# Extra score tiles through a cubic on GpSimd and VectorE, taken across segment borders, in a two-layer attention and MLP kernel

## The chip, the cores and the metric

The kernel runs on one core of a Trainium2 chip. The core's engines work at once, each through its own queue in order: TensorE (PE) for matrix products, ScalarE (ACT) for table functions, VectorE (DVE) and GpSimd (POOL) for elementwise work, SyncE (SP) for issuing DMAs. The metric is the device time of one execution in microseconds. Before the change the median of 3 runs is 1077.08 us (1075.46 to 1078.64).

## What is computed

Two layers, each an attention block and a mixer block, with residual sums around them; batch 1, sequence S = 2048, width D = 448, 16 heads of 28, inner width 1792, all in bf16.

```python
def _A_ref(x, wqkv, wo):                       # attention
    qkv = (x @ wqkv).reshape(B, S, 3, H, Dh).transpose(2, 0, 3, 1, 4)
    q, k, v = qkv[0], qkv[1], qkv[2]
    p = softmax(einsum("bhqd,bhkd->bhqk", q, k) * Dh ** -0.5)
    return einsum("bhqk,bhkd->bhqd", p, v).transpose(0, 2, 1, 3).reshape(B, S, D) @ wo

def _B_ref(x, w1, w2, w3, w4):                 # token mixer and MLP
    h = gelu(layernorm(x) @ w1)
    x1 = x + shift_four_groups(h, by=(1, -1, 2, -2)) @ w2
    return x1 + gelu(layernorm(x1) @ w3) @ w4

x = x + _A_ref(layernorm(x), A_wqkv, A_wo)
x = x + _B_ref(layernorm(x), B_w1, B_w2, B_w3, B_w4)
x = x + _A_ref(layernorm(x), A_wqkv, A_wo)     # the same weights again
x = x + _B_ref(layernorm(x), B_w1, B_w2, B_w3, B_w4)
```

Every score must go through an exponential: 2 x 16 x 2048 x 2048 of them. They are the heart of the change.

## The kernel before

**A planner writes the order.** The kernel is a set of Python generators (tasks) that yield operations with an estimated duration, and requests for resources: PSUM banks, scratch slots, events. A planner (`Sched`) simulates the five engines with these estimates, picks the next operation by start time and priority, and so fixes each engine's instruction order; waits between engines are semaphores. On the chip each engine follows its list. When PE would idle, the planner puts in filler matmuls (L1863) that keep the array busy and its clock up; `SC.idle_share(8.0)` is the share of filler in the last 8 us of the plan.

**Scores.** A segment (`segs`) is one query chunk, one group of four heads and a run of key tiles; there are 64, in the order of `ORDER`. In chunks 0 to 2 a query chunk has 512 columns and a key block (`kb`) is one key tile of 128; in chunks 3 and 4 it has 256 columns and a block holds two key tiles. Each block has four score tiles of 128x512, one a head: 2048 tiles in both layers. A segment of chunk 0 in layer 0 has 4, 4 and 8 blocks, one of chunks 1 and 2 has 16; in layer 1 chunks 0 and 1 are cut to 7, 4 and 5 blocks, chunk 2 has 16.

`t_scores` takes the tiles in order in units of alternately three and two, computes them on PE (L1292) into banks 0 to 2 or 3 to 4, and `t_exp` has ACT take the exponential of a whole unit in one instruction (L1447) into a slot of `PT`. `t_pv` multiplies with the values (`vaug`), two key blocks at a time, in order (L753), then VectorE copies the sum out (L1526, L1528) and `t_norm` divides by the row sums (L1541, L1552 and DMAs).

**Extra tiles.** A unit may carry one or two tiles more, taken from a block 5 or 6 ahead (`DLO`, `DHI`) of the same segment, if there is at least 3% filler (`FTH`), if the segment's share is not used up (`D_RATE` x 4 x blocks so far), and if a bank of b6 and b7, one of two `yd` slots and one of four `PD` slots are free at once. Such a tile goes to VectorE: `d_first` scales it out of PSUM to a fixed-point integer whose upper half is the exponent and whose lower half is the fraction (L1333), `d_chain` evaluates a cubic of the fraction in three instructions (L1354, L1356, L1358) with an fp32 buffer of `fb`, and a fourth (L1361) puts the exponent into the bits of the bf16 result in `PD`.

**Value slots.** `vaug` has 23 slots. Layer 0 uses 0 to 15; layer 1 uses 16 to 22 for key tiles 0 to 6 and 0 to 8 for the rest, so that its first keys and values can be computed while layer 0 runs. Slots 9 to 15 also hold the inner activations of two-tile MLP groups of layer 1.

**Other work on GpSimd and VectorE.** VectorE evacuates all projections from PSUM (L1102 keys, L1135 queries, L1180 values, L1813 MLP) and does normalisations; GpSimd squares keys and queries (L1088), computes row statistics (L945 to L947, L1627 to L1639, L1757, L1759), starts the gelu of the mixer (L1694, followed by L1695 to L1697 on VectorE and ACT), multiplies the attention output (L1552) and adds residuals (L1768).

The cost that the planner uses for a VectorE tile:

```python
DST = [('dve', 0.6), ('dve', 0.6), ('dve', 0.34), ('dve', 0.6)]
```

Of the kernel before, what the change touches and what calls it, by code (L numbers as in the profile page):

```python
# [511 lines left out]
DPRIO = 5  # L512
DST = [('dve', 0.6), ('dve', 0.6), ('dve', 0.34), ('dve', 0.6)]
DLO = 5
# [5 lines left out]
PE_NORM = {(0, 0): False, (0, 1): False, (0, 2): False, (0, 3): False, (0, 4): False, (1, 0): False, (1, 1): False, (1, 2): False, (1, 3): False, (1, 4): True}  # L520
# [24 lines left out]
def build_kernel(nc, A_x, A_wqkv, A_wo, B_x, B_w1, B_w2, B_w3, B_w4, out, n_layers=2):  # L545
# [20 lines left out]
    E0, E1, E2, E3 = 0.99992525, 0.69583285, 0.22606939, 0.07802301  # L566
    NPD = 4
# [56 lines left out]
    with st:  # L624
# [73 lines left out]
        RTN, TMP, T2, RIN = (sc[:, i, :] for i in range(4))  # L698
# [142 lines left out]
        def t_setup_pool():  # L841
# [13 lines left out]
            yield op("pool", 0.2, lambda e: e.memset(astat0[:, :], 0.0), writes=[("astat0",)])  # L855
            yield ("sig", ("ind",))
# [328 lines left out]
        def t_kv(L, c):  # L1185
            t0, n = KC[L][c]
            if L == 1 and c >= 2:
                yield ("wait", ("kvfree",))
            if L == 1 and c >= FASTKV:
# [136 lines left out]

        PDS = ["pd%d" % i for i in range(NPD)]
        YS = ["y0", "y1"]

        def d_first(blk, bank, ys, pd):  # L1330
            w = num1(ys)
            y = yd[:, w, :]
            yield op("dve", c_ps(512), lambda e: e.tensor_scalar(out=y, in0=ps[:, bi(bank), :], scalar1=SCALE * L2E * FS, scalar2=-126.0 * FS, op0=ALU.mult, op1=ALU.max),  # L1333
                     reads=[("ps", bi(bank))], writes=[("yd", w)], touch=[bank])
            yield ("rel", bank)
            yield ("spawn", d_chain(blk, ys, pd), DPRIO)

        at = [0, 0]

        def d_chain(blk, ys, pd):  # L1340
            si, kb, _ = blk
            w, s = num1(ys), home[blk][1]
            y = yd[:, w, :]
            lo = y.bitcast(U16).rearrange("p (n two) -> p n two", two=2)[:, :, 0]
            hi = y.bitcast(I16).rearrange("p (n two) -> p n two", two=2)[:, :, 1]
            pdt = PD[:, s, :]

            def urge():
                return 1.0 if at[0] > si or (at[0] == si and at[1] >= kb - DURG) else DPRIO

            fr = yield ("acq", FB, [("yd", w)])
            fk = ("fb", num1(fr))
            q = fb[:, num1(fr), :]
            yield op(DST[0][0], DST[0][1], lambda e: e.scalar_tensor_tensor(out=q, in0=lo, scalar=E2 / E3 * FS, in1=lo, op0=ALU.add, op1=ALU.mult),  # L1354
                     reads=[("yd", w)], writes=[fk], urge=urge)
            yield op(DST[1][0], DST[1][1], lambda e: e.scalar_tensor_tensor(out=q, in0=q, scalar=E1 / E3 * FS * FS, in1=lo, op0=ALU.add, op1=ALU.mult),  # L1356
                     reads=[("yd", w), fk], writes=[fk], urge=urge)
            yield op(DST[2][0], DST[2][1], lambda e: e.tensor_scalar(out=pdt, in0=q, scalar1=E3 / FS ** 3, scalar2=E0, op0=ALU.mult, op1=ALU.add),  # L1358
                     reads=[fk], writes=[("pd", s)], urge=urge)
            yield ("rel", fr)  # L1360
            yield op(DST[3][0], DST[3][1], lambda e: e.scalar_tensor_tensor(out=pdt.bitcast(I16), in0=hi, scalar=128.0, in1=pdt.bitcast(I16), op0=ALU.mult, op1=ALU.add),  # L1361
                     reads=[("yd", w), ("pd", s)], writes=[("pd", s)], urge=urge)
# [3 lines left out]
        def t_scores():  # L1366
# [9 lines left out]
            while pos < len(stream):  # L1376
# [23 lines left out]
                si, kb0, _ = un[-1]  # L1400
                at[0], at[1] = si, kb0
                L, ch, g = segs[si][0:3]
                nkb = len(seg_kb[si])
                rate = DRATE(L, ch, g)
                if rate and CHUNKS[L][ch][1] == 4 and SC.idle_share(8.0) >= FTH:
                    for kb in range(kb0 + DLO, min(kb0 + DHI, nkb)):
# [3 lines left out]
                        if taken.get(si, 0) >= rate * (kb + 1) * 4:  # L1410
                            continue
                        if any(("k", L, g, kc_of(L, kt)) not in SC.events for kt in seg_kb[si][kb]):
                            break
                        got = yield ("try", [MISC[0:2], YS, PDS])
# [3 lines left out]
                        home[blk] = ("pd", int(got[2][2:]))  # L1418
                        taken[si] = taken.get(si, 0) + 1
# [39 lines left out]
        def t_pv():  # L1459
            yield ("wait", ("start",))  # L1460
            yield ("acq", ["b5"])
            for si in range(len(segs)):
# [7 lines left out]
                for k0 in range(0, len(kbs), PVB):  # L1470
# [6 lines left out]
                    for kb in batch:  # L1477
                        for i, kt in enumerate(kbs[kb]):
                            vs = vslot(L, kt)
                            for j in range(4):  # L1480
                                key, s = home[(si, kb, j)]
                                buf = PD if key == "pd" else PT
# [4 lines left out]
                        for j in range(4):  # L1487
                            key, s = home[(si, kb, j)]
                            if key == "pd":
                                yield ("rel", "pd%d" % s)  # L1490
# [198 lines left out]
        def t_tanh(L, t0, grp, z, NW, hk):  # L1689
            yield ("wait", ("hz", L, t0, grp))  # L1690
            fr = yield ("acq", FB, hk)
            fk = ("fb", num1(fr))
            f = fb[0:112, num1(fr), 0:NW]
# [4 lines left out]
            yield ("rel", fr)  # L1698
            yield ("sig", ("hA", L, t0, grp))

# [71 lines left out]
        def t_mixB(L, tiles, direct, pr):  # L1772
# [20 lines left out]
            elif side:  # L1793
                yield ("wait", ("kvfree",))
# [6 lines left out]
            late = []  # L1801
            for fch in range(14):
# [5 lines left out]
                if direct or ("tail",) in SC.events:  # L1808
# [6 lines left out]
                yield ("spawn", later([ev], b, [("h2", L, tiles[0], fch)]), 1.5)  # L1815
            yield ("rel", x_)
            for fch in range(14) if not direct else ():
                yield ("wait", ("h2", L, tiles[0], fch))
# [5 lines left out]
            for i, t in enumerate(tiles):  # L1824
# [4 lines left out]
                for fch in range(14):  # L1829
                    if direct:  # L1830
                        yield ("wait", ("h2", L, tiles[0], fch))
# [69 lines left out]
        SC.spawn(t_third(), 3)  # L1901
        SC.spawn(t_final(), 9)
# [58 lines left out]
```

## Time and profile before

| | |
|---|---|
| median of 3 runs | 1077.08 us |
| the profiled execution | 1079.42 us, span 1077.7 us, mean granted clock 0.995 |
| instructions on VectorE, ACT, GpSimd | 1234, 919, 506 |
| GpSimd's two-input rows of 512 columns (mean) | L1552 1308 ns, L1694 1244 ns, L1088 1074 and 1050 ns |
| GpSimd's row statistics | 209 to 615 ns each |
| exponentials of three tiles, of two | 1548 ns x402, 1126 ns x402 (they overlap each other) |
| layer 1's first key projection, evacuated by VectorE | 272.98 to 284.03 us |
| layer 1's second one | 420.22 to 436.15 us |

In the profile's rows "busy" is the union of a group's spans and the mean is one instruction's duration. In the table of stretches each row has a stretch, its length, busy time and count of PE, PE's weight loads, DVE, ACT and POOL, the granted clock, the DMA share and GB/s. Lines are those of the kernel's file.

### The profile page before, as it was taken

The numbers are of one execution on the slowest core, as the hardware profiler recorded it, in microseconds if no ns is written. First come the engines' busy times: TensorE is split into PE (matmuls) and PEld (weight loads), VectorE is DVE, ScalarE is ACT, GpSimd is POOL, SyncE is SP. The second block draws the span as 40 slices with busy tenths as digits, with TensorE's granted clock in tenths as the row PEclk, the third lists the DMA queues.
The fourth block names the chain that finished last, engine by engine and source line by source line (L and its number), as shares of the span: only waits on it lengthen the run. The fifth ranks groups of instructions, "written<-read, shape, count | busy, mean of one in ns | idle before, by whom it ended". The sixth has DMA issues, their size and how long they took to land.

```text
span 1077.7 us, 35124 instructions
## 1 busy us (share of the span) xinstructions
PE 1006.0 (93%) x15918; PEld 420.7 (39%) x15921; DVE 637.4 (59%) x1234; ACT 1017.9 (94%) x919; POOL 312.7 (29%) x506
## 2 busy tenths in 40 slices
PE   6899999999999999899999999999999999999998
PEld 2333443443333344343433333343333433444464
DVE  8776679836568526766356643515695394554551
ACT  6898999999999999999999999999999999999951
POOL 2244125301254014452032201102743030432130
PEclk9999999999999999999999999999999999999999
DMA  4547221103111022220221132423311110220000
GB/s 114 138 111 211 78 56 33 27 12 91 32 31 32 12 70 65 49 36 23 43 77 41 43 93 84 132 69 100 79 27 22 46 36 12 53 58 16 12 11 33
DMA packets 92614, 62.26 MB, mean 58 GB/s; under 512 B 64688, under 2 KB 82368, under 8 KB 92464
## 3 DMA queue, kind: packets, MB, share of 16 engines
q1 hardware_dynamic: 89088, 51.92, 18.7%
q0 software_dynamic: 3376, 8.09, 2.7%
q8 instruction: 125, 2.05, 0.8%
q14 instruction: 25, 0.20, 0.1%
HBM read 27.12 MB, written 15.71 MB: 40 GB/s over the span
## 4 chain that ended last, share of the span: by engine, by line
ACT 73%; PE 17%; DVE 6%; DMA 2%; issue 1%; POOL 1%; SPq 0%; DVEq 0%
ACT PT L1447 66%; PE ps L762 10%; PE ps L1292 4%; ACT h2T L1822 4%; PE ps L753 3%; ACT fb L1696 1%; ACT L1822 1%; DMA rT<-ub 1%; ACT L1447 1%; DVE fb L1356 1%; DVE rT L1541 0%; DVE yd L1333 0%; DVE PD L1361 0%; DVE fb L1354 0%; DMA PT<-in_A_wqkv_dram 0%
## 5 line engine op out<-in xcount | busy, mean ns | idle before, releaser
L1447 ACT ACTIVATE PT<-ps 128x1536 bf16<-128x1536 f32 (+1 forms) x805 | 921.7, 1336 | 17.9 <-PE ps L1292 17.1
L1292 PE MATMUL ps<-qT,kT 32*128 32x512 bf16 (+1 forms) x2560 | 315.2, 340 | 33.2 <-ACT PT L1447 24.0
L753 PE MATMUL ps<-PT,vaug 128*32 128x512 bf16 (+1 forms) x2523 | 251.8, 342 | 0.0
L1292 PEld LDWEIGHTS ps<-qT,kT 32*128 32x128 bf16 x2560 | 80.7, 91 | 309.5 <-ACT PT L1447 279.9
L1863 PE MATMUL ps<-ident 128*32 128x256 bf16 x3688 | 165.3, 274 | 3.7 <-POOL ident L842 1.5
L762 PE MATMUL ps<-xT,w 128*32 128x512 bf16 (+2 forms) x1600 | 127.7, 360 | 2.6 <-DVE h2T L1813 1.6
L1863 PEld LDWEIGHTS ps<-ident 128*32 128x32 bf16 x3688 | 105.0, 96 | 31.0 <-issue 11.9
L1813 DVE CAST h2T<-ps 128x512 bf16<-128x512 f32 (+2 forms) x112 | 67.9, 606 | 81.0 <-PE ps L762 73.7
L762 PE MATMUL ps<-w,h2T 128*32 128x448 bf16 x1512 | 103.1, 360 | 10.2 <-ACT h2T L1822 9.8
L753 PEld LDWEIGHTS ps<-PT,vaug 128*32 128x32 bf16 x2523 | 74.5, 95 | 94.6 <-issue 81.5
L1552 POOL TENSOR_TENSOR otn<-ub,fb 128x512 bf16<-128x512 f32 (+1 forms) x36 | 40.3, 1119 | 175.6 <-DMA fb<-rscr 172.5
L1088 POOL TENSOR_TENSOR sq<-kT 128x512 bf16<-128x512 bf16 (+2 forms) x32 | 30.0, 939 | 121.5 <-DVE kT L1102 120.9
L1694 POOL TENSOR_TENSOR fb<-hT 112x512 f32<-112x512 bf16 (+1 forms) x36 | 37.7, 1049 | 83.3 <-DVE hT L1676 73.5
L762 PEld LDWEIGHTS ps<-xT,w 128*32 128x32 bf16 (+1 forms) x1600 | 44.2, 95 | 41.8 <-issue 19.3
L762 PEld LDWEIGHTS ps<-w,h2T 128*32 128x32 bf16 x1512 | 41.7, 97 | 45.8 <-issue 16.4
L1768 POOL TENSOR_TENSOR x_res<-x_res,x1b 128x448 f32<-128x448 f32 x32 | 40.2, 1262 | 23.9 <-DVE xn L959 23.8
L1333 DVE TENSOR_SCALAR yd<-ps 128x512 int32<-128x512 f32 x37 | 24.9, 679 | 32.9 <-PE ps L1292 32.7
L1541 DVE RECIPROCAL rT<-rT 16x128 f32<-16x128 f32 (+1 forms) x36 | 33.5, 932 | 17.1 <-DMA rT<-ub 17.1
L762 PE MATMUL ps<-kT,w 128*32 128x512 bf16 (+2 forms) x576 | 40.0, 360 | 2.5 <-DVE qT L1164 1.4
L1822 ACT ACTIVATE h2T<-h2T 128x7168 bf16<-128x7168 bf16 (+2 forms) x8 | 42.0, 5244 | 0.1
L1526 DVE COPY ub<-ps 128x512 f32<-128x512 f32 (+1 forms) x40 | 23.3, 582 | 30.7 <-PE ps L753 30.1
L762 PE MATMUL ps<-xT,wq_pad 128*32 128x512 bf16 x448 | 40.2, 396 | 0.6 <-DVE kmaxc L1113 0.3
(164 smaller groups left out, 1168.3 us busy)
## 6 DMA issues: line engine op xcount, KB each, us to landing
uscr<-ub SPq DMA_DIRECT2D x24, 256.0 KB, 2.0
ub<-uscr SPq DMA_DIRECT2D x24, 256.0 KB
fb<-rscr SPq DMA_DIRECT2D x24, 256.0 KB
xnd<-xn SPq DMA_DIRECT2D x28, 128.0 KB, 2.0
x_res<-in_A_x_dram POOLq DMA_DIRECT2D x16, 224.0 KB, 4.3
xd<-x_res SPq DMA_DIRECT2D x16, 224.0 KB, 2.2
x_res<-xd SPq DMA_DIRECT2D x16, 224.0 KB, 3.6
out_dram<-obf SPq DMA_DIRECT2D x16, 112.0 KB
```

The costliest lines, as they stand in the source:

```text
L753: return lambda e: e.matmul(out=out, lhsT=lhsT, rhs=rhs, start=start, stop=stop, **kw)
L762: r.append(e.matmul(out=out[c:c + w, :], lhsT=lhsT[:, c:c + w], rhs=rhs, start=start, stop=stop, tile_position=(0, c)))
L1088: return op("pool", 0.15 + NW * 0.0018, lambda e: e.tensor_tensor(out=sq[:, si, 0:NW], in0=src, in1=src, op=ALU.mult), reads=rk, writes=[( ...
L1292: yield op("pe", max(0.055, 0.22 / nc_ * NW / 512.0), lambda e, i=i, kc=kc, j=j, g=g, a=a, NW=NW, bank=bank: e.matmul(out=ps[:, bank, i * ...
L1447: yield op("act", 0.06 + n * w * 0.000833, lambda e, bk=bk, s0=s0, n=n, w=w: e.activation(out=PT[:, s0:s0 + n, 0:w], in_=ps[:, bk[0]:bk[0] ...
L1541: yield op("dve", 0.86, lambda e: e.reciprocal(out=rT[0:4 * n, :], in_=rT[0:4 * n, :]), reads=[("rT",)], writes=[("rT",)])
L1552: yield op("pool", 0.2 + NW * 0.0021, lambda e: e.tensor_tensor(out=otn[:, g, 0:NW], in0=u, in1=rb[:, 0:NW], op=ALU.mult), reads=[uk, fk], ...
L1694: yield op("pool", 0.2 + NW * 0.00165, lambda e: e.tensor_tensor(out=f, in0=z, in1=z, op=ALU.mult), reads=hk, writes=[fk])
L1768: yield op("pool", 1.2, lambda e: e.tensor_tensor(out=X, in0=X, in1=X1, op=ALU.add), reads=[xk, ("x1b", s)], writes=[xk], deps=[nop_])
L1813: ev = op("dve", c_ps(NW), lambda e, fch=fch, b=b: e.tensor_copy(out=hb[:, fch, 0:NW], in_=ps[:, bi(b), 0:NW]), reads=[("ps", bi(b))], wri ...
L1822: yield op("act", c_act(nl * NW), lambda e: e.activation(out=hb[:, 0:nl, 0:NW], in_=hb[:, 0:nl, 0:NW], func=ACT.Gelu_apprx_tanh), reads=al ...
L1863: return [e.matmul(out=ps[32 * c:32 * c + 32, bi(b), 0:256].rearrange("p (a n) -> p a n", n=128), lhsT=ident[:, 32 * c:32 * c + 32], rhs=i ...
```

## The change

1. **A second kind of extra tile**, `"pool"`. `d_first` is as before. Then GpSimd adds a constant to the fraction, squares, adds a constant column (`dcol`, a new memset) and multiplies, all in fp32; VectorE turns the exponent half into the result's bits with one tensor_scalar and adds the polynomial with one scalar_tensor_tensor. The integer slot serves as fp32 scratch.
2. **Choice of tiles.** For each unit the planner tries pool tiles first, 9 or 10 blocks ahead, at a rate of 0.1, with at most two in flight and only if GpSimd's planned end is at most 1 us past its clock; then VectorE tiles, 5 or 6 ahead, at the old rates. Both now count on into the next segment (`DSEG = 1`). Rates count for each kind by itself.
3. **More scratch.** `xtra` adds two integer slots, one fp32 buffer and one result slot, in value slots 16 to 22 until segment 20 starts, and in 9 to 15 from the end of layer 0 until segment 54 starts. `t_extra` then takes all four back and, for the first set, writes the padding columns again with two GpSimd memsets. Layer 1's first two key and value projections wait for this (`("xdone", 0)`), and layer 1's two-tile MLP groups for `("xdone", 1)`.
4. **A split gelu** for the MLP (`t_tanh_w`), used where `TANHW` is not 0. All its values are 0. `t_tanh`'s body moves to `tanh_gelu`, with the same operations.

```diff
+PLAG = 4
+PTS = 1.5
+DSEG = 1
+PFLY = 2
+PBACK = 1.0
+PRATE = {(0, 0): 0.1, (0, 1): 0.1, (0, 2): 0.1, (0, 3): 0.1, (1, 0): 0.1, (1, 1): 0.1, (1, 2): 0.1}
+XSHUT = (20, 54)
...
+TANHW = {(0, 0): 0, (0, 3): 0, (0, 7): 0, (0, 11): 0, (0, 13): 0, (1, 0): 0, (1, 3): 0, (1, 7): 0, (1, 11): 0}
...
             if L == 1 and c >= 2:
                 yield ("wait", ("kvfree",))
+            if L == 1 and c < 2:
+                yield ("wait", ("xdone", 0))
...
+        def xtra(kind):
+            for ph, base in ((0, 16), (1, 9)):
+                if ("xopen", ph) in SC.events and ("xshut", ph) not in SC.events:
+                    return {"y": ["yv%d" % base, "yv%d" % (base + 2)], "f": ["fv%d" % (base + 4)], "pd": ["pv%d" % (base + 6)]}[kind]
+            return []
+
+        def t_extra(ph, base):
+            yield ("wait", ("vinit",) if ph == 0 else ("kvfree",))
+            yield ("sig", ("xopen", ph))
+            yield ("wait", ("segstart", XSHUT[ph]))
+            yield ("sig", ("xshut", ph))
+            for r in ("yv%d" % base, "yv%d" % (base + 2), "fv%d" % (base + 4), "pv%d" % (base + 6)):
+                yield ("acq", [r])
+            if ph == 0:
+                pads = vaug[:, base:base + 7, :].rearrange("p t (h r) -> p (t h) r", r=32)
+                wk = [("vaug", base + k) for k in range(7)]
+                yield op("pool", 1.0, lambda e: e.memset(pads[:, :, 28:32], 0.0), writes=wk)
+                yield op("pool", 0.5, lambda e: e.memset(pads[:, :, 28:29], 1.0), writes=wk)
+            yield ("sig", ("xdone", ph))
...
+            fr = yield ("acq", xtra("f") + FB, yk)
+            q, fk = fbuf(fr)
+            D_ = DST
+            if blk in bypool:
+                w = y.bitcast(FP32)
+                yield op("pool", PTS, lambda e: e.tensor_scalar(out=q, in0=lo, scalar1=G1 * FS, scalar2=None, op0=ALU.add), reads=yk, writes=fk, urge=urge)
+                yield op("dve", 0.4, lambda e: e.tensor_scalar(out=pdt.bitcast(I16), in0=hi, scalar1=128.0, scalar2=16128.0 + 60.0, op0=ALU.mult, op1=ALU.add), reads=yk, writes=[pk], urge=urge)
+                yield op("pool", 1.2, lambda e: e.tensor_tensor(out=w, in0=q, in1=q, op=ALU.mult), reads=fk, writes=yk, urge=urge)
+                yield op("pool", 1.2, lambda e: e.tensor_tensor(out=w, in0=w, in1=dcol[:, 0:1].to_broadcast([128, 512]), op=ALU.add), reads=yk + [("dcol",)], writes=yk, urge=urge)
+                yield op("pool", 1.2, lambda e: e.tensor_tensor(out=w, in0=w, in1=q, op=ALU.mult), reads=yk + fk, writes=yk, urge=urge)
+                yield ("rel", fr)
+                yield op("dve", 0.6, lambda e: e.scalar_tensor_tensor(out=pdt.bitcast(I16), in0=w, scalar=G0 * 128.0 / FS ** 3, in1=pdt.bitcast(I16), op0=ALU.mult, op1=ALU.add), reads=yk + [pk], writes=[pk], urge=urge)
+                yield ("rel", ys)
+                flying[0] -= 1
+                yield from finished(blk)
+                return
...
-                if rate and CHUNKS[L][ch][1] == 4 and SC.idle_share(8.0) >= FTH:
-                    for kb in range(kb0 + DLO, min(kb0 + DHI, nkb)):
+                for kind in ("pool", "dve"):
+                    if kind == "pool" and SC.cur["pool"] > SC.clock + PBACK:
+                        continue
+                    if SC.idle_share(8.0) < FTH:
+                        continue
+                    lag = PLAG if kind == "pool" else 0
+                    for ahead in range(DLO + lag, DHI + lag):
+                        si, kb = si0, kb0 + ahead
+                        while si < len(segs) and kb >= len(seg_kb[si]):
+                            kb -= len(seg_kb[si])
+                            si += 1
+                        if si > si0 + DSEG or si >= len(segs):
+                            break
+                        L, ch, g = segs[si][0:3]
+                        rate = (DRATE(L, ch, g) if kind == "dve" else PRATE.get((L, ch), 0)) if CHUNKS[L][ch][1] == 4 else 0
+                        if not rate or (kind == "pool" and flying[0] >= PFLY):
+                            break
                         js = [j for j in range(4) if (si, kb, j) not in home and j not in [b_[2] for b_ in blks]]
                         if taken.get((si, kb), 0) >= DPK or not js or len(blks) >= 4:
                             continue
-                        if taken.get(si, 0) >= rate * (kb + 1) * 4:
+                        if taken.get((si, kind, 0), 0) >= rate * (kb + 1) * 4:
                             continue
                         if any(("k", L, g, kc_of(L, kt)) not in SC.events for kt in seg_kb[si][kb]):
                             break
-                        got = yield ("try", [MISC[0:2], YS, PDS])
+                        if si > si0 and (("q", L, CHUNKS[L][ch][0] // 4, g) not in SC.events or (not segs[si][5] and ("qp", si) not in SC.events)):
+                            break
+                        got = yield ("try", [MISC[0:2], xtra("y") + YS, xtra("pd") + PDS])
...
+            soft = TANHW.get((L, tiles[0]), 0) and not direct
```

## The prediction

> **What bounds the kernel now.** I read the page's busy table first, then the chain of waits, then the costliest groups, then tables of stretches, and last the timeline around GpSimd's operations.
>
> ```profile
> PE 1006.0 (93%) x15918; PEld 420.7 (39%) x15921; DVE 637.4 (59%) x1234; ACT 1017.9 (94%) x919; POOL 312.7 (29%) x506
> ...
> ACT 73%; PE 17%; DVE 6%; DMA 2%; issue 1%; POOL 1%; SPq 0%; DVEq 0%
> ...
> L1447 ACT ACTIVATE PT<-ps 128x1536 bf16<-128x1536 f32 (+1 forms) x805 | 921.7, 1336 | 17.9 <-PE ps L1292 17.1
> ```
>
> ScalarE (ACT) is the bound: 94% busy, 73% of the chain, and the exponentials of L1447 are 921.7 us of its 1017.9. They waited for scores 17.1 us in all. PE's 93% is not a second bound, since L1863 is filler that keeps its clock up. The other 60 us of ACT's idle time lie mostly at the start and in the last 54 us, where only MLP work is left; an extra score tile touches neither.
>
> What is a tile worth? In the chain's own list 42 exponentials in a row, alternately of three and two tiles, took 47.56 us from 95.76 us on: 1.132 us for 2.5 tiles, **0.45 us a tile**. The 805 instructions hold about 2011 of the 2048 tiles; the other 37 went to VectorE:
>
> ```profile
> L1356 DVE SCALAR_TENSOR_TENSOR fb<-fb,yd 128x512 f32<-128x512 f32 x37 | 30.4, 827 | 0.4
> ...
> L1354 DVE SCALAR_TENSOR_TENSOR fb<-yd 128x512 f32<-128x512 uint16 x37 | 27.7, 763 | 0.4
> ...
> L1361 DVE SCALAR_TENSOR_TENSOR PD<-yd,PD 128x512 int16<-128x512 int16 x37 | 25.7, 700 | 0.7
> L1333 DVE TENSOR_SCALAR yd<-ps 128x512 int32<-128x512 f32 x37 | 24.9, 679 | 32.9 <-PE ps L1292 32.7
> ...
> L1358 DVE TENSOR_SCALAR PD<-fb 128x512 bf16<-128x512 f32 x37 | 16.1, 440 | 0.6
> ```
>
> Where can more be taken? The planner wants at least 3% filler in the last 8 us. The first table has all engines, the second the filler's (L1863) alone:
>
> ```profile
> 104.00:390.00 286.00, 268.73 (x4283) 111.12 (x4283) 187.83 (x310) 284.84 (x248) 79.92 (x117) 1.00 0.17 43
> 390.00:510.00 120.00, 113.81 (x1991) 48.74 (x1987) 76.69 (x148) 118.45 (x111) 50.03 (x89) 0.99 0.22 52
> ...
> 702.00:732.00 30.00, 29.22 (x530) 14.33 (x532) 6.21 (x8) 30.00 (x28) 2.55 (x2) 1.00 0.34 96
> ...
> 770.00:896.00 126.00, 117.47 (x1789) 45.62 (x1784) 88.58 (x154) 123.31 (x110) 41.40 (x59) 0.99 0.14 32
> ```
> ```profile
> 104.00:390.00 286.00, 76.95 (x1688) 48.48 (x1688) 1.00 0.17 43
> 702.00:732.00 30.00, 18.18 (x374) 10.83 (x372) 1.00 0.34 96
> ...
> 770.00:896.00 126.00, 18.55 (x452) 12.16 (x452) 0.99 0.14 32
> ```
>
> Columns are length, then busy time and count of PE, PEld, DVE, ACT, POOL. Two thirds of the filler lies in 104 to 390 us and in 702 to 732, and ACT is full there: room to take tiles, and a tile taken shortens the stretch. In 702 to 732 VectorE and GpSimd stand idle, and no tile was taken: these are segments of 5 key blocks, in which "5 or 6 blocks ahead in the same segment" does not exist. In 104 to 390 VectorE is already 66% busy.
>
> **The Trainium skill.** "SBUF — State Buffer", Who interferes with whom: a VectorE instruction with two SBUF inputs, or in a 2-port mode, and a GpSimd instruction that reads SBUF exclude each other for the whole instruction. The trace agrees:
>
> ```profile
> 187.30 1.80 DVE L1697 SCALAR_TENSOR_TENSOR hT<-fb,hT 112x512 bf16<-112x512 f32 x1
> ```
> ```profile
> 187.29 1.27 POOL L1552 TENSOR_TENSOR otn<-ub,fb 128x512 bf16<-128x512 f32 x1 [3.09 <-DVE hT L1676]
> ```
>
> The VectorE operation began with a GpSimd one and took 1.80 us, the 1.27 in front of it and something over its usual 0.68. "GPSIMD Engine Reference", 3.1: about 2.6 cycles an element for two-input arithmetic, some 1.1 us for 512 at 1.2 GHz; here L1552 has a median of 1.27 us, L1088 and L1694 1.04. "VectorE: DVE Perf Modes", tier table: an fp32 tensor_scalar from SBUF runs at twice the rate; L1358's median of 0.42 us beside L1356's 0.68 agrees.
>
> **The change, part by part.**
>
> *A GpSimd tile.* Removed from ACT: 0.45 us. Added on GpSimd: one tensor_scalar from strided 16-bit halves, which no row shows; nearest are an fp32 tensor_tensor (1.27) above and a plain copy of 448 (L888, 0.56) below; I take 1.3. Then three fp32 tensor_tensors: a square (L1694, 1.04), an add of a broadcast column (unknown, 1.04 to 1.4, I take 1.27) and a product (1.27). Sum 4.9 us, 4.2 to 5.5. On VectorE: the PSUM evacuation and the last scalar_tensor_tensor at their pace of 0.6 each (instructions overlap: starts at 192.07 and 192.67 us) and a tensor_scalar of 0.35 to 0.6: 1.6 us, against 2.8 for a VectorE tile. Scores and PV matmuls stay the same.
>
> *How many.* Of 599 exponentials of four-tile chunks I count 304 in the timeline with three or more filler groups in the 8 us before: 156 in 104 to 390 us, 50 around 770 to 896 us. Before, the five-block look-ahead within a segment left 162 of them eligible, and 37 tiles were taken. For GpSimd: two in flight, chosen 9 or 10 blocks ahead, none while its plan is over 1 us late. It is 28% busy there, so 4.9 us of work takes 4.9/0.72 = 6.8 us, with the gaps of the chain about 8. 156 x 1.14 us = 178 us give 22 tiles, 57 us give 7, and some 3 elsewhere: **32**, 18 to 45. For VectorE: caps of 3 or 4 a segment in 104 to 390 us, mostly reached, +6; the borders open 702 to 770 us, +10; the last stretch +4: **20**, 8 to 35. Together 52 x 0.45 = **-23.4 us**, -12 to -36.
>
> *What is given back on VectorE and GpSimd.* In 104 to 390 us VectorE gets 22 x 1.6 + 6 x 2.8 = 52 us. Lock losses: the 26 chains there average 784, 854, 447 and 686 ns against free medians 682, 684, 421, 691, so 0.29 us a chain or 7.6, and some 12 with the hT rows. GpSimd goes from 80 to 80 + 22 x 4.9 = 188 us there, 2.4 times, and there are a fifth more chains: 12 becomes some 35, +23. VectorE: 188 + 52 + 23 = 263 of 286 - 13 = 273 us, 96%. The cover over these edits is VectorE's idle third, and it is nearly used up. What queues behind a blocked VectorE operation are the PSUM evacuations; PE waits for their banks in order, the next scores are behind them, and ACT waits for those. I charge **+7 us**, 0 to 25. GpSimd's small row statistics (0.2 to 0.6 us each) also stand behind an operation of up to 1.3 us; they feed normalisations that are not ACT's, so that is in the 7.
>
> *The moved wait.* Layer 1's first key projection ran at 273 to 284 us (its 128x384 evacuations) beside filler. It now waits until the scratch slots are free, at about 391 us (segment 20 starts and segment 19's PV ends), with its key, square and value matmuls (4 x 4 x 4, 4 x 4 and 3 x 4 x 4 of them, some 6 us of PE), evacuations, transposing load on SP's queue and GpSimd squares. From 390 to 510 us PE works 113.8 of 120 us, with only 7.1 of filler. Bounds 0 (390 to 442 us has slack) and 6; **+3**. It stays ahead of segment 28, which starts at about 510 us, so nothing else should wait.
>
> *The rest.* Two memsets on GpSimd (1.5 us by the plan; L932's took 1.6) at 391 us, off the chain; a column memset at the start. The MLP's split tanh is switched off: every value of TANHW is 0. A different order re-draws the places where ACT waits (17.1 us before): 0 to +6, below nothing too; **+2**.
>
> Sum: -23.4 + 7 + 3 + 2 = **-11.4 us**. The profiled execution took 1079.4 us (span 1077.7), so 1068; its distance from the median of 1077.1 is 2.3, so **1066 us**.
>
> **Rivals.** *More fits (0.12).* If GpSimd's operations run at the low bounds and borders open more, 75 tiles for 4 us given back: -34 + 4 = -30, 1047 us. For it: the idle 702 to 732 us. Against: PD slots, of which a GpSimd tile holds one for ten blocks, 18 us.
> *No change (0.13).* 25 tiles, 11 us, given back by the same waits: 1077. For it: banks b6 and b7 are shared with all evacuations, and 37 of 162 were taken before.
> *VectorE becomes the bound (0.29), slower.* The planner prices the operations without the lock. With 30 GpSimd and 12 more VectorE tiles in 104 to 390 us: 188 + 48 + 34 + 45 lock = 315 us of work in 286 - 19 = 267. If three quarters of the excess of 48 come out as waits, that is +36, with 5 for the moved projection, against 31 gained by some 69 tiles: +10, 1087 us. It decides once VectorE passes 100% of that stretch, some 24 GpSimd and 8 VectorE tiles.
>
> **How the numbers follow.** The likeliest case (0.46) is 1066, with a range of its own from 1055 to 1073. Faster by over 0.3% (about 3.2 us, what a measurement here can tell from no change): the first two cases, 0.58; within it 0.13; slower 0.29. The range takes in the larger gain and most of the slower case: 1046 to 1090.
>
> **What would show it.** Right: fewer L1447 tiles by about 52, some 32 new chains on GpSimd, ACT still near 100% in 104 to 390 us, GpSimd above half there. Wrong: ACT waiting for scores well over 17 us, with VectorE above 95% and its two-input operations at 1 us or more; or a count of new tiles under 25 or over 75; or a new hole before segment 28 behind the late key projection.

## The result, and the profile after

| | before | after |
|---|---|---|
| median | 1077.86 us of 4 runs (1075.46 to 1081.47) | 1142.07 us of 4 runs (1139.33 to 1145.69) |
| ratio | 1 | 1.0595 (1.0546 to 1.0643) |
| profiled execution, its span | 1079.42, 1077.7 us | 1145.69, 1144.0 us |
| mean granted clock of TensorE | 0.995 | 0.958 |
| score tiles off ACT: by GpSimd's chain, by VectorE's | 0, 37 | 34, 45 |

The change makes the kernel about 64 us slower. The forecast of 1066 us, with a range up to 1090, was wrong in sign and in range. The page of the kernel after, with its rows of busy time, granted clock and shares of the chain, and the exponentials' group:

```profile
PE 1021.0 (89%) x15394; PEld 410.4 (36%) x15397; DVE 776.8 (68%) x1374; ACT 1005.6 (88%) x904; POOL 506.9 (44%) x645
...
PEclk9999899888989999999999999998989999999899
...
ACT 46%; PE 27%; DVE 22%; issue 2%; DMA 1%; POOL 1%; SPq 0%; DVEq 0%
...
L1531 ACT ACTIVATE PT<-ps 128x1536 bf16<-128x1536 f32 (+1 forms) x788 | 907.8, 1299 | 95.4 <-PE ps L1304 91.5
```

ACT did get less work: 788 exponentials instead of 805, 12.3 us less busy. But its wait for scores rose from 17.1 to 91.5 us, 74 us more. Less the 12.3 us, that is 62 of the 66 us between the two profiled spans. VectorE and PE took over 26 of the 27 points that ACT lost in the shares of the chain. The slices with an 8 in the clock row are new. Seven of the eight lie where extra tiles are, the last (1058 to 1087 us) behind them. The same stretches as before, in the same columns (length, then busy time and count of PE, PEld, DVE, ACT, POOL, clock, DMA share, GB/s):

```profile
104.00:390.00 286.00, 237.86 (x3346) 89.91 (x3338) 239.56 (x339) 237.35 (x207) 204.56 (x205) 0.91 0.15 40
390.00:510.00 120.00, 109.70 (x1800) 42.98 (x1794) 70.56 (x124) 112.99 (x98) 45.77 (x67) 0.97 0.20 49
...
770.00:896.00 126.00, 107.67 (x1373) 35.49 (x1376) 108.38 (x159) 107.43 (x96) 87.72 (x104) 0.91 0.27 59
```

A stretch is one of time, not of work: segment 20 starts at 387 us before and at 425 us after. In the first row ACT fell from 284.8 to 237.4 us of 286. No engine is full there: PE 83%, VectorE 84%, ACT 83%, GpSimd 72%. The kernel became slower without any engine becoming the bound, and that is what has to be explained. VectorE's chain instructions, then GpSimd's (count, busy time, mean ns of one, idle before):

```profile
L1428 DVE SCALAR_TENSOR_TENSOR PD<-yd,PD 128x512 int16<-128x512 int16 x21 | 21.0, 1000 | 0.4
L1423 DVE SCALAR_TENSOR_TENSOR fb<-fb,yd 128x512 f32<-128x512 f32 x19 | 18.8, 992 | 0.2
L1421 DVE SCALAR_TENSOR_TENSOR fb<-yd 128x512 f32<-128x512 uint16 x19 | 18.2, 956 | 0.1
L1416 DVE SCALAR_TENSOR_TENSOR PD<-vaug,PD 128x512 int16<-128x512 f32 x16 | 18.0, 1125 | 0.0
```
```profile
L1413 POOL TENSOR_TENSOR vaug<-vaug,sc 128x512 f32<-128x512 f32 x19 | 23.6, 1242 | 0.6
L1410 POOL TENSOR_SCALAR fb<-yd 128x512 f32<-128x512 uint16 x11 | 19.4, 1760 | 26.5 <-DVE yd L1383 26.3
...
L1414 POOL TENSOR_TENSOR yd<-yd,fb 128x512 f32<-128x512 f32 x11 | 16.5, 1503 | 0.5
L1412 POOL TENSOR_TENSOR yd<-fb 128x512 f32<-128x512 f32 x11 | 14.0, 1276 | 5.1 <-DVE PD L1411 5.0
```

L1421, L1423 and L1428 are the old L1354, L1356 and L1361, which had means of 763, 827 and 700 ns; now they are near 1 us. Nothing in them changed; what runs beside them on GpSimd did.

**One place, followed from end to end.** Timelines of VectorE, GpSimd, PE and ACT after (start, length, engine, line, in square brackets the idle time before and its releaser):

```profile
232.86 1.52 DVE L1416 SCALAR_TENSOR_TENSOR vaug<-vaug 128x512 int16<-128x512 f32 x1
234.31 1.52 DVE L1428 SCALAR_TENSOR_TENSOR PD<-vaug,PD 128x512 int16<-128x512 int16 x1
235.75 1.74 DVE L1780 SCALAR_TENSOR_TENSOR hT<-fb,hT 112x512 bf16<-112x512 f32 x1
```
```profile
232.62 1.22 POOL L1412 TENSOR_TENSOR yd<-fb 128x512 f32<-128x512 f32 x1
233.91 1.36 POOL L1413 TENSOR_TENSOR yd<-yd,sc 128x512 f32<-128x512 f32 x1
235.36 1.59 POOL L1414 TENSOR_TENSOR yd<-yd,fb 128x512 f32<-128x512 f32 x1
```
```profile
233.72 0.37 PE L771 MATMUL ps<-w,hT 112*32 112x448 bf16 x4
237.55 0.56 PE L771 MATMUL ps<-w,hT 112*32 112x448 bf16 x4 [3.46 <-DVE hT L1780]
238.04 1.03 PE L1304 MATMUL ps<-qT,kT 32*128 32x512 bf16 x3
```
```profile
230.82 4.66 ACT L1531 ACTIVATE PT<-ps 128x1536 bf16<-128x1536 f32 x4
239.11 1.45 ACT L1531 ACTIVATE PT<-ps 128x1536 bf16<-128x1536 f32 x1 [3.63 <-PE ps L1304]
```

Three VectorE operations in a row start while a GpSimd operation runs and end after it, at 1.5 to 1.7 us each instead of some 0.68. Each starts late because the one before was held up. The third, L1780, makes the `hT` that an MLP matmul waits for; the scores of L1304 stand behind this matmul in PE's order. PE waits 3.46 us, ACT 3.63. Then the table of stretches around this place:

```profile
232.00:236.60 4.60, 1.92 (x23) 0.53 (x21) 4.60 (x4) 3.48 (x4) 4.44 (x4) 1.00 0.14 46
236.60:243.40 6.80, 5.85 (x44) 1.35 (x48) 6.77 (x10) 2.71 (x3) 3.23 (x3) 0.50 0.02 8
243.40:255.00 11.60, 10.98 (x182) 4.52 (x174) 11.32 (x20) 11.60 (x11) 9.47 (x12) 1.00 0.19 36
```

For 6.8 us PE is granted half its clock, and ACT is busy for 2.71 of them. Of its 4.1 us of idle time here, 2.5 are still the wait of 3.63 us, and the rest are waits for scores at half clock. The Trainium skill, "TensorE: Matmul & The Clock Gate", Part 1, says that an idle activity window of some 3.4 us puts the clock back to half rate; here the drop comes at 236.64 us, during a PE wait of 3.46 us, and lasts 6.8.

From 100 us to the end of the last segment there were 3 such drops with 10.2 us at half clock before, and 18 with 95.6 us after. ACT was idle for 91.0 us in that window after, and 45.0 of them lie in the stretches at half clock; before it was 8.9, with 1.4 in such stretches. That they lie there does not make the clock their cause: as in the place above, part of such idle time is the wait that came with the drop. Nor does a drop need one long wait. After, all 5 PE waits of over 3 us came with a drop, but that is 5 of the 18; in the 3.4 us ahead of 12 of the 18 PE was busy for less than 40% of the time, mostly in pieces.

Where is ACT idle? With the exponentials of the trace counted off in the plan's order, it is idle for 53 us more than before in segments 0 to 19, for nothing more in segments 20 to 43 (0.5 us, before 3.0), and for 30 us more in segments 44 to 63. GpSimd's tiles lie in the first and the last of these.

### The profile page after: what moved, and what is told of

It reads as the page before. It is cut to its first block, busy times and chain, and to the rows that moved or that the text cites. A ratio compares the mean times of both kernels' runs of the same rounds, so it can differ in the third digit from the quotient of the medians.

```text
span 1144.0 us, 34384 instructions
## 1 busy us (share of the span) xinstructions
PE 1021.0 (89%) x15394; PEld 410.4 (36%) x15397; DVE 776.8 (68%) x1374; ACT 1005.6 (88%) x904; POOL 506.9 (44%) x645
## 4 chain that ended last, share of the span: by engine, by line
ACT 46%; PE 27%; DVE 22%; issue 2%; DMA 1%; POOL 1%; SPq 0%; DVEq 0%
ACT PT L1531 40%; PE ps L771 14%; PE ps L1304 6%; PE ps L762 6%; ACT h2T L1928 3%; DVE fb L1423 2%; DVE PD L1428 2%; DVE fb L1421 1%; DVE PD L1425 1%; DVE yd L1383 1%; DVE PD L1416 1%; PE ps L1969 1%; DVE vaug L1383 1%; ACT fb L1779 1%; DVE PD L1411 1%
## 5 line engine op out<-in xcount | busy, mean ns | idle before, releaser
L1531 ACT ACTIVATE PT<-ps 128x1536 bf16<-128x1536 f32 (+1 forms) x788 | 907.8, 1299 | 95.4 <-PE ps L1304 91.5
L1304 PE MATMUL ps<-qT,kT 32*128 32x512 bf16 (+1 forms) x2560 | 318.5, 350 | 35.9 <-ACT PT L1531 28.6
L1304 PEld LDWEIGHTS ps<-qT,kT 32*128 32x128 bf16 x2560 | 79.6, 92 | 313.8 <-ACT PT L1531 254.8
L771 PE MATMUL ps<-xT,w 128*32 128x512 bf16 (+1 forms) x1984 | 156.7, 370 | 13.7 <-DVE h2T L1913 4.5
L1969 PE MATMUL ps<-ident 128*32 128x256 bf16 x3164 | 144.0, 280 | 11.5 <-DVE yd L1383 5.3
L1969 PEld LDWEIGHTS ps<-ident 128*32 128x32 bf16 x3164 | 89.4, 98 | 42.6 <-issue 10.7
L771 PEld LDWEIGHTS ps<-xT,w 128*32 128x32 bf16 x1984 | 56.5, 97 | 62.2 <-issue 28.5
L771 PE MATMUL ps<-xT,wq_pad 128*32 128x512 bf16 x512 | 47.8, 410 | 0.5 <-DVE kmaxc L1123 0.3
L771 PE MATMUL ps<-wo_pad,otn 128*32 128x448 bf16 x512 | 41.3, 370 | 6.0 <-DVE x_res L1690 6.0
L771 PE MATMUL ps<-w,hT 112*32 112x448 bf16 x512 | 41.1, 380 | 4.6 <-DVE hT L1780 3.5
L1928 ACT ACTIVATE h2T<-h2T 128x5376 bf16<-128x5376 bf16 (+3 forms) x8 | 41.5, 5189 | 0.1
L1098 POOL TENSOR_TENSOR sq<-qT 128x512 bf16<-128x512 bf16 x28 | 32.2, 1154 | 19.5 <-DVE qT L1145 11.6
```

The source lines that it names most:

```text
L771: r.append(e.matmul(out=out[c:c + w, :], lhsT=lhsT[:, c:c + w], rhs=rhs, start=start, stop=stop, tile_position=(0, c)))
L1098: return op("pool", 0.15 + NW * 0.0018, lambda e: e.tensor_tensor(out=sq[:, si, 0:NW], in0=src, in1=src, op=ALU.mult), reads=rk, writes=[( ...
L1304: yield op("pe", max(0.055, 0.22 / nc_ * NW / 512.0), lambda e, i=i, kc=kc, j=j, g=g, a=a, NW=NW, bank=bank: e.matmul(out=ps[:, bank, i * ...
L1531: yield op("act", 0.06 + n * w * 0.000833, lambda e, bk=bk, s0=s0, n=n, w=w: e.activation(out=PT[:, s0:s0 + n, 0:w], in_=ps[:, bk[0]:bk[0] ...
L1928: yield op("act", c_act(nl * NW), lambda e: e.activation(out=hb[:, 0:nl, 0:NW], in_=hb[:, 0:nl, 0:NW], func=ACT.Gelu_apprx_tanh), reads=al ...
L1969: return [e.matmul(out=ps[32 * c:32 * c + 32, bi(b), 0:256].rearrange("p (a n) -> p a n", n=128), lhsT=ident[:, 32 * c:32 * c + 32], rhs=i ...
```

## The experiments

The first theory, **A**: VectorE, held up by GpSimd's wide operations (those on all 512 columns), delays what PE waits for in order, and so ACT; the half clock makes it worse. Rivals: **B**, the late key projection of layer 1 costs the time; **C**, tiles across borders disturb the order; **D**, GpSimd is simply too busy, so that its chains and its row statistics come late. All ratios are against the kernel before on the same chip.

### Leaving parts out

**No GpSimd tiles.**

```diff
-PRATE = {(0, 0): 0.1, (0, 1): 0.1, ...}
+PRATE = {}
```

> The changed kernel with PRATE empty: no tile goes to GpSimd; the borders, the extra scratch and the moved key projection stay. Theory 1 (GpSimd's new operations lock VectorE out[...], VectorE fills up, PE waits for it, ACT waits for PE): 1060 to 1095 us, ACT's wait for scores (L1531 <- PE) under 40 us, means of L1421, L1423, L1428 near 0.75 us. Theory 2 (the other parts: borders, banks b6 and b7, moved projection, redrawn order): stays at 1110 or more. Theory 3 (less filler lets PE's clock drop): stays slow with a clock under 0.97.

1090.43 us, 1.0104 (1.0058 to 1.0150), clock 0.978, with 70 tiles on VectorE. Five sixths of the loss is gone with the GpSimd tiles, though VectorE carries 25 tiles more than after. ACT's wait for scores is 28.2 us.

**No borders.** `DSEG = 0`.

> The changed kernel with DSEG = 0: GpSimd tiles stay, but none is taken from the next segment (the plan has 18 GpSimd and 31 VectorE tiles then, for 34 and 45). Theory 1: the loss goes with GpSimd's new work, so about half of it, 1095 to 1125 us. Theory 2 with the borders as the cause: 1075 to 1090 us.

1122.27 us, 1.0414 (1.0388 to 1.0439): 18 GpSimd and 31 VectorE tiles, and still 4% slower. Most of the loss does not need the borders, which goes against C as the main cause. With fewer GpSimd tiles there is less loss, though each of these runs also has an order of its own.

**Scratch alone.** `PRATE = {}` and `DSEG = 0`.

> The changed kernel with PRATE empty and DSEG = 0: what is left of the change is the extra scratch in the value slots, the per-kind count, the late key projection of layer 1 and a redrawn order. Theories 1 and 3: within 1% of before, 1070 to 1090 us. Theory 2 with the moved projection as the cause: 1095 or more, with ACT's waits before segment 28.

1086.54 us, 1.0090 (1.0054 to 1.0126), 41 tiles. With neither GpSimd tiles nor borders, some 10 us of loss are left.

**The late projection alone.** As the last, and no scratch is handed out:

```diff
 def xtra(kind):
+    return []
```

> No GpSimd tiles, no borders, no scratch: only the late key projection of layer 1 (its wait and the two memsets on GpSimd) against the kernel before, with 38 VectorE tiles for 37. If the late projection is what made the scratch version slower: 1083 to 1092 us. If it was the scratch (more VectorE tiles at once): 1075 to 1080 us.

1093.87 us, 1.0141 (1.0107 to 1.0174), 38 tiles. The wait by itself costs about 1.4%, 15 us, where I had charged 3. It is in the plan already: the planner's own estimate rises from 1061.7 to 1077.1 us, and in segments 28 to 35, which need the keys, ACT is idle for 7.2 us (before 1.1). So B is real in this order, and would be a quarter of the loss. In the kernel after, ACT is idle for 0.3 us in the same segments, so no wait of that kind shows there.

**Borders alone.** No GpSimd tiles, no scratch; the early key projection is back:

```diff
+PRATE = {}
 def xtra(kind):
+    return []
...
-yield ("wait", ("xdone", 1))
+yield ("wait", ("kvfree",))
...
-SC.spawn(t_extra(0, 16), 3)
-SC.spawn(t_extra(1, 9), 3)
+SC.events.add(("xdone", 0))
+SC.events.add(("xdone", 1))
```

> Only the look-ahead across borders for VectorE tiles: no GpSimd tiles, no scratch, the key projection where it was before (61 VectorE tiles for 37). If tiles are worth 0.45 us each and borders are harmless: 1066 to 1072 us. If what is gained before layer 1's last keys is given back in the wait for them: 1074 to 1082 us. If VectorE tiles cost more than they bring: above 1083 us.

1078.61 us, 1.0000 (0.9983 to 1.0018), 61 tiles. 24 tiles more than before are worth 24 x 0.45 = 11 us on ACT, and none of it is seen in the time. C falls as a loss, but the expected gain isn't there either; it is looked for below.

**GpSimd tiles without scratch.** The same edits with `PRATE` as in the change.

> GpSimd tiles and borders stay, but no scratch in value slots and so no late key projection (the plan has 43 GpSimd and 13 VectorE tiles, and VectorE's planned work is as before the change, 560 us for 558). If the scratch or the late projection made the loss: 1085 us or less. If GpSimd's work beside VectorE makes it: 1110 us or more, though VectorE has no more to do by the plan than before.

1098.32 us, 1.0197 (1.0177 to 1.0217), 43 GpSimd and 13 VectorE tiles. It lies between what the theories said. GpSimd is busier than after (525.8 against 506.9 us), but with 32 VectorE chains fewer, VectorE (676.2 against 776.8 us) offers less to hold up. ACT waits 38.1 us for scores.

### The same order, other operations on GpSimd

These three have the instruction order of after, instruction by instruction; only what GpSimd's four operations do is changed. They separate A from D and from all that lies in the order.

**Narrow:** each of the four works on 8 of 512 columns, so the chain computes almost nothing.

```diff
-e.tensor_tensor(out=w, in0=w, in1=q, op=ALU.mult)
+e.tensor_tensor(out=w[:, 0:8], in0=w[:, 0:8], in1=q[:, 0:8], op=ALU.mult)
```

> The changed kernel with the same order on every engine, but the four GpSimd operations of a tile work on 8 of 512 columns, so that part of the cubic is left out for these tiles. Theory 1: VectorE's two-input operations return to about 0.7 us, VectorE's busy time falls by 80 us or more, and the time to 1050 to 1090 us. Theory 2: the order and all transfers are the same, so 1120 or more. Theory 3: the filler is the same, so the clock stays under 0.97 and the time at 1110 or more.

1083.45 us, 1.0055 (1.0036 to 1.0074). Its busy row, and the rows of VectorE's chain:

```profile
PE 993.5 (92%) x15394; PEld 407.2 (38%) x15397; DVE 714.8 (66%) x1374; ACT 1001.7 (93%) x904; POOL 366.6 (34%) x645
```
```profile
L1428 DVE SCALAR_TENSOR_TENSOR PD<-yd,PD 128x512 int16<-128x512 int16 x21 | 16.0, 764 | 0.4
L1423 DVE SCALAR_TENSOR_TENSOR fb<-fb,yd 128x512 f32<-128x512 f32 x19 | 14.5, 763 | 0.2
L1421 DVE SCALAR_TENSOR_TENSOR fb<-yd 128x512 f32<-128x512 uint16 x19 | 13.2, 693 | 0.1
```

The same 1374 VectorE instructions take 62.0 us less, and ACT's wait for scores falls from 91.5 to 37.9 us. So 5.4 of the 6 points come from the width of the GpSimd operations. The order, the late projection and what was gained on ACT leave 0.6 between them.

**As long, but without reading tiles:** powers on 5 to 8 columns of a small tile of ones, about as long as the real operations.

```diff
-e.tensor_tensor(out=w, in0=w, in1=q, op=ALU.mult)
+e.tensor_tensor(out=w[:, 0:7], in0=ones_f[:, 0:7], in1=ones_f[:, 0:7], op=ALU.pow)
```

> The changed kernel with the same order; each GpSimd operation of a tile is replaced by a power over 5 to 8 columns of constants, about as long as the operation it stands for (the cubic of these tiles is left out). In the traces so far VectorE operations that met such small powers were not held up (excess within 0.01 us), while those that met a wide GpSimd operation lost 0.3 to 0.9 us. If VectorE being held up is the cause: 1080 to 1095 us with VectorE below 725 us busy. If GpSimd being busy is the cause: 1125 us or more at VectorE below 725 us.

1098.75 us, 1.0227 (1.0183 to 1.0270). Its busy row, and two rows each of VectorE's and GpSimd's groups:

```profile
PE 998.4 (91%) x15394; PEld 409.0 (37%) x15397; DVE 719.1 (66%) x1374; ACT 1002.8 (91%) x904; POOL 515.3 (47%) x645
```
```profile
L1421 DVE SCALAR_TENSOR_TENSOR fb<-yd 128x512 f32<-128x512 uint16 x19 | 13.6, 714 | 0.1
L1423 DVE SCALAR_TENSOR_TENSOR fb<-fb,yd 128x512 f32<-128x512 f32 x19 | 13.1, 691 | 0.2
```
```profile
L1410 POOL TENSOR_TENSOR fb<-ones_f 128x8 f32<-128x8 f32 x22 | 39.9, 1815 | 23.8 <-DVE yd L1383 22.1 <-DVE vaug L1383 1.8
L1414 POOL TENSOR_TENSOR vaug<-ones_f 128x7 f32<-128x7 f32 x19 | 31.3, 1645 | 0.4
```

GpSimd is busier than after, VectorE's operations are back at 0.7 us, and 3.7 of the 6 points are gone (1.0595 to 1.0227). That is A, about 40 us. What is left between this run and the narrow one, 1.7 points or 18 us, is D: GpSimd's time alone.

**Memsets:** each of the four becomes a memset of 1.0 or 1.85 us.

> The changed kernel with the same order, but each GpSimd operation of a tile is replaced by a memset of about its length (bytes or bf16 over the same buffers), so that the cubic of these tiles is left out: GpSimd is as busy as before, but reads nothing from SBUF. If the lock[...] is the cause: VectorE's two-input operations near 0.7 us, 1080 to 1095 us, close to the narrow version. If it is GpSimd being busy (row statistics and squares queue behind the chains): 1125 or more, with GpSimd near 500 us. If the 2-port operations on VectorE (L1425, L1411) are blocked by writes too: in between, with L1425 above 0.8 us.

1131.64 us, 1.0481 (1.0435 to 1.0527). VectorE's groups:

```profile
L1425 DVE TENSOR_SCALAR PD<-fb 128x512 bf16<-128x512 f32 x26 | 27.8, 1069 | 0.5
L1411 DVE TENSOR_SCALAR PD<-vaug 128x512 int16<-128x512 int16 x16 | 17.5, 1093 | 0.1
...
L1421 DVE SCALAR_TENSOR_TENSOR fb<-yd 128x512 f32<-128x512 uint16 x19 | 13.1, 688 | 0.1
```

I had meant it as "busy, but without the lock", and it isn't that: VectorE stays at 775.0 us, but other operations pay. The two-input ones are free (L1421 at 688 ns), the tensor_scalars of 0.42 us go to 1.07. The Trainium skill, "SBUF — State Buffer", Who interferes with whom, says that a two-input VectorE operation contends only with GpSimd operations that read SBUF, and one in a 2-port mode with any. So the time of this run, which lies where I had expected it for a busy GpSimd, doesn't tell A from D; the powers do. Here are the pairs of operations, by the GpSimd operation that was running when a VectorE operation of a tile's chain began. Each entry is the mean excess over the median of the same VectorE line with GpSimd idle, and the number of cases:

| GpSimd | two-input on VectorE | tensor_scalar on VectorE |
|---|---|---|
| wide tensor_tensor of a tile (after) | +0.71 us (45) | +0.58 (18) |
| wide tensor_scalar of a tile (after) | +0.10 (18) | +0.39 (20) |
| memset (this run) | 0.00 (55) | +1.00 (24) and +0.86 (14), for two lines |
| powers on 5 to 8 columns (the powers run) | +0.01 (85) | 0.00 (47) |

The 0.71 is most of what the GpSimd operation still had to run, 0.91 us in the mean. The second row is the exception: the GpSimd tensor_scalar reads SBUF and yet hardly holds up two-input operations. Why, these runs don't show.

### Would a better plan do?

**Priced by what was measured:** the planner's costs for VectorE's chain 1.0, 1.0, 0.7 and 1.0 us, for GpSimd's 1.7, 1.2, 1.2 and 1.5, and for VectorE's part of a GpSimd tile 0.6 and 1.0.

> The changed kernel planned with prices nearer to the measured ones (VectorE's chain operations 1.0, 1.0, 0.7, 1.0 us for 0.6, 0.6, 0.34, 0.6; GpSimd's 1.7 and 1.5 for 1.5 and 1.2). The plan then has 24 GpSimd and 38 VectorE tiles. If the loss is the gap between the plan's prices and the chip: 1085 to 1105 us, ACT's wait for scores below 50 us. If VectorE has no room for such tiles at any price, or the order matters little: 1115 us or more.

1119.26 us, 1.0393 (1.0369 to 1.0416), with 24 GpSimd and 38 VectorE tiles; ACT waits 48.8 us for scores. It is better than after, and worse than I expected. The planner's own estimate is now 1094.2 us, 32 above the 1061.7 before; for the change it was 1052.2. By the profiled spans the chip is slower than the estimate by 24 us here, by 16 before and by 92 after. So the prices close most of the gap between plan and chip, and most of the loss that is left stands in the plan itself: the planner takes a tile when its rules allow it, and doesn't ask whether it pays.

**Borders late only:** as the run with borders alone, with borders crossed in segments 43 to 50.

```diff
-if si > si0 + DSEG or si >= len(segs):
+if si > si0 + (1 if 43 <= si0 < 51 else 0) or si >= len(segs):
```

> As the borders-only version, but borders are crossed only between segments 43 and 51, behind the wait for layer 1's last keys, where VectorE and GpSimd stood idle before (48 VectorE tiles for 37). If a tile behind that wait keeps its gain: 11 x 0.45 = 5 us faster, 1070 to 1075 us. If the gain is lost at the next dependence (the MLP that must end before the last chunks' work, or the tail): 1076 to 1080 us.

1075.07 us over 22 runs, 0.9980 (0.9964 to 0.9995), 48 tiles. It is the best version, by about 2 us of the 5 that 11 tiles are worth, within what I call no change.

**The same with GpSimd tiles there**, eight of them, looked for one block further ahead than VectorE's (`PLAG = 1`) and only in segments 43 to 50.

> Extra tiles across borders, GpSimd's included (8 of them), only between segments 43 and 51, where VectorE and GpSimd stood idle before; no scratch, early projection. If GpSimd tiles are harmless where VectorE has room: as the late-borders version, 1070 to 1077 us. If they always cost more than they bring: 1080 us or more.

1079.62 us, 1.0024 (1.0012 to 1.0037), 48 tiles. It falls between the two expectations. It is 0.4 points, some 5 us, slower than the run with late borders, with intervals that don't meet: even where GpSimd and VectorE stood idle, eight GpSimd tiles in place of VectorE tiles gained nothing and rather cost. What of this is the redrawn order isn't separated.

### What the half clock costs by itself

The kernel before, in its own order, with filler matmuls 16 columns wide instead of 256; VectorE and GpSimd are left as they are.

```diff
-return [e.matmul(out=ps[..., 0:256]..., rhs=ident[...].to_broadcast([128, 2, 128]), ...)
+return [e.matmul(out=ps[..., 0:16], rhs=ident[:, 0:16], ...)
```

> The kernel before with the same order on every engine, but its filler matmuls 16 columns wide for 256: the filler's place stays, PE is idle in most of it; nothing is left out of the result. If PE's clock falls to half after idle stretches and this alone starves ACT: clock under 0.93, ACT's wait for scores over 40 us, 1100 us or more, though no transfer, VectorE or GpSimd operation has changed. If PE at half clock still feeds ACT (then the clock of the changed kernel is only a sign, not a part of its loss): 1090 us or less at a clock under 0.95.

1116.53 us, 1.0358 (1.0319 to 1.0397). Two rows of its page:

```profile
PE 1004.2 (90%) x15918; PEld 391.1 (35%) x15921; DVE 639.0 (57%) x1234; ACT 1025.1 (92%) x919; POOL 312.3 (28%) x506
...
PEclk9899988799896988989899999968989999978989
```

VectorE and GpSimd are as before, only the clock fell, to 0.905, and ACT's wait for scores rose to 47.3 us. It has 212 us at half clock, 200 more than before, for 39 us: 0.20 us for each, in the mean over places that are not those of after. PE isn't the bound of this kernel, and still its clock is paid for. At that rate the 84 us more at half clock after are worth some 17 us (an estimate), which are a part of A's and D's share, not beside it.

## Why the prediction was wrong

**Where the 64 us come from**, by runs with one instruction order: 40 us from VectorE held up by wide GpSimd operations (after to powers), 18 us from GpSimd's time (powers to narrow), 6 us left (narrow to before). By the intervals the first two are good to some 5 to 7 us. The last holds a gain: in the narrow run too, ACT's busy time is 16 us less than before (1001.7 against 1017.9; 42 tiles at 0.45 would be 19). So some 22 us are given back in it.

**The count of tiles** was near. 32 GpSimd tiles were forecast, 34 were taken, 23 of them in 104 to 390 us where I had 22. VectorE got 8 more, not 20. Together 42 against 52, which is 4.5 us of the error.

**The costs of one tile** were near as well: GpSimd's four operations took 5.6 us against 4.9. At their shortest they are 1.48, 1.03, 1.03 and 1.25, sum 4.8, so the rest is probably GpSimd held up by VectorE in its turn, which isn't shown.

**The step that failed** is "What is given back on VectorE and GpSimd", in its last part: "I charge **+7 us**, 0 to 25". The runs put 58 us there, 40 for the hold-up and 18 for GpSimd's time. VectorE's work was forecast well, in part by luck. Up to segment 20 I had 240 us of work and 23 of new hold-up, 263 in all. From 104 us to the start of segment 20 VectorE was busy for 261 us after and 215 in the narrow run: less work, since VectorE got one tile fewer there and not six more, and twice the hold-up, 46 us. The mistake was to turn this into a wait by utilisation: 96% of the stretch, so nearly all of it still fits. It didn't fit. The stretch that was to shrink to 273 us took 321, VectorE was busy for 81% of it, and ACT, which was idle for 1.2 us from 104 to 390 us before, was idle there for 48.6. A hold-up of 0.7 us, three times in a row, delays one instruction by more than 2 us, whatever the mean; PE waits for that instruction in order, with the scores behind it. And when PE stands idle so much, 3.4 or 6.8 us at half clock follow, which I had left out altogether, although the filler is there for that very purpose.

**The moved wait**, "**+3**", was too small where it stands alone: it cost 15 us there, with its redrawn order. The projection came at 406.9 us in the narrow run, by its first key evacuation, instead of 273. I had looked for a hole before segment 28. There is none after: segment 28 starts at 551.7 us, and ACT is idle for 0.4 us in all of segments 20 to 35. So what the wait costs in the change, if anything, lies elsewhere and isn't shown.

**The gain that vanishes** in the narrow run goes in good part at one place: layer 1's last keys. Timelines of ACT and PE in that run, then the first key evacuation there (L1112) and in the kernel before (L1102):

```profile
678.99 7.05 ACT L1531 ACTIVATE PT<-ps 128x1024 bf16<-128x1024 f32 x6
695.84 5.54 ACT L1531 ACTIVATE PT<-ps 128x1024 bf16<-128x1024 f32 x5 [9.80 <-PE ps L1304]
```
```profile
686.10 1.59 PE L1969 MATMUL ps<-ident 128*32 128x256 bf16 x44
689.15 0.83 PE L771 MATMUL ps<-kT,wk_pad 128*32 128x384 bf16 x16 [1.47 <-issue]
...
695.41 0.60 PE L1304 MATMUL ps<-qT,kT 32*128 32x512 bf16 x5
```
```profile
690.03 0.62 DVE L1112 TENSOR_SCALAR kT<-ps,cols 128x384 bf16<-128x384 f32 x1 [2.67 <-PE ps L771]
680.80 0.61 DVE L1102 TENSOR_SCALAR kT<-ps,cols 128x384 bf16<-128x384 f32 x1
```

Segment 43 ends at 686.0 us there and at 693.7 before, so 8 us are gained by then. But the scores of the next segment need keys that come out of layer 0's MLP. Their evacuations begin at 690.0 us in the narrow run, and at 680.8 before, where they were in time and ACT went through without a gap. PE first has only filler, then the projection, and ACT waits 9.80 us. Segment 44 starts at 695.8 us instead of 692.4: the 8 us are lost, and 3 more because the keys came later, for a reason that isn't shown. After has the same hole, 9.65 us up to 743.9. By segments, ACT in the narrow run is idle for 9 us more than before in 0 to 19, for nothing more in 20 to 43, and for 16 more in 44 to 63, these 9.80 included.

So work taken off ACT ahead of this point is worth nothing unless the keys are there in time. In the run without GpSimd tiles their first evacuation came at 681.6 us, 8 us earlier than in the narrow run, and segment 44 started at 688.1. Behind this point part of the gain stays: the late borders, with half as many added tiles as borders everywhere, kept 2 of 5 us. I had priced a tile at 0.45 us everywhere.

**The rivals.** "VectorE becomes the bound" (0.29) had the mechanism, with its waits behind held-up evacuations. Its size was +10, and its condition, VectorE past 100%, never came about. "More fits" and "No change" fall with the sum. Of the signs listed, ACT waiting well over 17 us and two-input operations near 1 us came; VectorE above 95% and the hole before segment 28 didn't. The condition that "decides once VectorE passes 100%" is the same mistake as in the failed step: the waits came at 81%.

**Slips in the readings**, on which the forecast doesn't hang: the filler of 104 to 390 and 702 to 732 us is 95 of 165 us, 58% and not two thirds. ACT's idle time was 60 us in all, with the 17.1 for scores among them. And the held-up operation at 187.30 us took 1.80 us; less the 1.27 in front that leaves 0.53, which is under the usual 0.68 and not over it.

What isn't settled: how the 22 us of the narrow run split between the redrawn order, the late projection and the late keys, as each run that drops one of them has another order. Nor was GpSimd's 18 us divided between late chains and late row statistics.

## What to carry to other kernels

An operation put on GpSimd costs, beside its own time, what it holds up on VectorE: here 0.7 us for each two-input operation that met a wide tensor_tensor, and this adds up along a chain that PE waits for in order, long before VectorE is full; mean utilisation doesn't show it. A PE wait can cost more than itself: all 5 of over 3 us came here with 3.4 or 6.8 us at half clock. And work taken off the bound pays only up to the next dependence that doesn't come earlier with it: find that dependence before pricing the gain.

## What the runs showed of the hardware

- GpSimd's tensor_scalar on 128x512 strided 16-bit halves to fp32 (1.48 us at its shortest, 1.70 to 1.92 in the mean) is slower than its fp32 tensor_tensor (1.03 to 1.25 at the shortest). Adding a broadcast column costs no more than squaring.
- It held up two-input VectorE operations by only 0.10 us in the mean (18 cases), while the faster tensor_tensors held them up by 0.71 (45 cases).
- Memsets on GpSimd held up VectorE's tensor_scalars by 0.9 to 1.0 us in the mean and two-input operations not at all; powers on a few columns, 1.2 to 1.9 us long, left VectorE's chain at 0.7 us.
- Filler 16 columns wide doesn't keep PE's clock as filler of 256 does: 0.905 against 0.995 in the same order, and 0.20 us lost for each us at half clock.
